# Attention scores as four float32r products of rounded parts and rests over 128 rows, softmax sums divided out of the rows of values, last layer's rows transposed by DMA

## Chip, cores and metric

The kernel runs on one core of one Trainium2 chip, in one launch. The metric is device microseconds of that core. PE is the matrix engine (PEld its weight loads), DVE the vector engine, ACT the scalar engine, POOL the GpSimd engine, SP the queue that issues every DMA.

## What is computed

The reference, cut to what matters:

```python
B, H, S, D = 4, 8, 576, 64
scores = 1 / sqrt(D) * q @ k.T                          # per batch and head, 576x576
kth = the 32nd largest score of each row
attn = exp(where(scores >= kth, scores, -1e9) - max)
attn = attn / (sum(attn) + 1e-9);  out = attn @ v
x = rows of out, heads side by side                      # 2304x512
x = (sigmoid(x @ w_gate) * (x @ w_val)) @ w_out          # 512 -> 1536 -> 512
h = x @ w_in;  solu = h * softmax(h)                     # 512 -> 1024
out = (layer_norm(solu) * g_ln) @ w_out2                 # 1024 -> 512
```

All inputs and the output are float32. The choice of the 32nd largest score makes the scores need close to full float32 precision.

## The kernel before, in words

The 2304 token rows are cut into 18 chunks of 128 rows: per batch four chunks of 128 rows (main), and two chunks that each hold the last 64 rows of two batches (remainder). A chunk's attention is four steps, 72 in all; a step takes two heads of a main chunk, or four heads of 64 remainder rows.

A step goes so. PE makes the scores in two halves of 288 keys (`scores`, L628 for main chunks, L625 for remainder ones) into the PSUM tile ps. The contraction is over 64 rows only: two heads lie in the upper and the lower half of the 128 rows, and their float32 products run at the same time in two (remainder: four) parts of the array. In the trace each float32 product is two records, so a half of a main step is 4 records of L628 and a half of a remainder step 8 of L625. ACT copies ps to s (L634), DVE folds the halves by maximum and minimum (L639, L643) into w and finds the 32nd largest value in four rounds of top eight (L653 MAX8, L657 MATCH_REPLACE8). ACT masks and takes exponentials (L675, L680, with the row sums in sm). POOL adds 1e-9 to the sum (`total1`, L684), DVE inverts it (L688), ACT rounds the normalised row to half precision (`prob_hi`, L701), POOL normalises the row in float32 (`norm`, L693) and subtracts the rounded part (`prob_lo`, L705). One DMA transposes both halves (L712, tile et), and PE multiplies them with the values (`attend`, L727).

After four steps the chunk's sums of values, av, are scaled and split in two float16 parts xt (L753, then L771 on POOL or L764 on DVE). The three dense layers work with three float16 products for each float32 one: gate and value groups pg, pv (L863), px (L909), ph (L946), po (L1044), each in groups of 12 products of 128 columns or 3 of 512. The second rests are made by POOL from a float32 copy in chunks 0 to 3, and by DVE straight from PSUM (`lower`, L764) in chunks 4 to 17, which the constant DIRECT lists. Before the last layer the rows e (128x1024) are turned: PE transposes them in eight float32 blocks (`turn`, L1018, tile pl), ACT and DVE split them (L1023, L764).

The weights come in as doubles and are rebuilt to float32 in the first 150 us by DVE (L424 to L430), ACT and POOL, then split in float16 halves.

The order on each engine is written out by a planner (class Order): every piece of work has an engine, a booked cost, a rank, its needs, and buffers that it takes and frees (BUFS gives the number of each). The table SHIFT moves the ranks by key. The planner plays the program through with these costs and issues the instructions in the order found; each engine runs its own list in order. SP has one list too, with loads, transposes and stores in it.

Of the kernel before, what the change touches and what calls it, by code (L numbers as in the profile page):

```python
# [10 lines left out]
F32 = mybir.dt.float32  # L11
F16 = mybir.dt.float16
# [9 lines left out]
P = 128  # L22
# [18 lines left out]
DIRECT = tuple(range(4, 18))  # L41
# [4 lines left out]
BUFS = dict(s=4, ks=5, v=4, q=2, w=4, et=2, ps=1, pt=1, av=1, pm=4, xt=1, gh=1, two=3, big=2, xf=1, x2=1)  # L46
# [9 lines left out]
ADDED = tuple(range(24))  # L56
STAGED = 36
SHIFT = {
# [75 lines left out]
def terms(name):  # L134
# [6 lines left out]
    if k in ("kd", "vd", "vn", "vh", "vl"):  # L141
        return [(k, 1.0), (("b", name[1]), 1.0)]
# [176 lines left out]
def body(ctx, tc, q_main, q_rem, k_dup, v_pad, w_gate, w_val, w_out1, w_in, w_out2, g_ln, out):  # L319
# [251 lines left out]
    for x, ch in enumerate(chunks):  # L571
        ch["x"] = x
# [617 lines left out]
```

## Time and profile before

| | |
|---|---|
| median of 3 runs | 1004.01 us (1003.17 to 1004.04) |
| the profiled execution | 1002.34 us |
| its span, first to last instruction | 1000.6 us |
| mean granted clock of TensorE | 0.973 of full speed |
| PE, PEld busy | 883.0 us (88%), 668.1 us (67%) |
| DVE busy | 865.0 us (86%) |
| ACT busy | 724.4 us (72%) |
| POOL busy | 569.6 us (57%) |
| chain of work that ended last | PE 75%, DVE 13%, ACT 6%, DMA 3% |

The shares are means over three parts: the first 150 us, in which weights are made ready, a long middle in which attention and dense layers run side by side, and a tail of dense layers alone.

### The profile page before, as it was taken

What the parts mean: (1) busy time and instruction counts of PE and PEld (TensorE: products, weight loads), DVE (VectorE), ACT (ScalarE), POOL (GpSimd) and SP (SyncE); (2) the same over time, 40 slices, a digit from 0 to 9 for tenths busy, and PEclk for the clock granted to TensorE, in tenths of its full rate; (3) what the DMA queues carried; (4) which work ended last, traced back from release to release, by engine and by line L of the source; (5) the groups of instructions that cost most, each with busy time, mean ns of one, the idle gap of its engine ahead of it and who ended that gap; (6) DMA issues with size and microseconds to landing.
All of it is one profiled execution on the core that took longest, in us unless ns stands there. A gap on an engine that the chain in (4) does not pass through costs nothing.

```text
span 1000.6 us, 29578 instructions
## 1 busy us (share of the span) xinstructions
PE 883.0 (88%) x12052; PEld 668.1 (67%) x12052; DVE 865.0 (86%) x2321; ACT 724.4 (72%) x1319; POOL 569.6 (57%) x824
## 2 busy tenths in 40 slices
PE   1343249899999999999999999999999999999995
PEld 1112138777786868786877777676868687877962
DVE  7999999999999999999899999999999999823232
ACT  4998999888789878667797776777987677632221
POOL 6876787786657766555475645645673546530000
PEclk9999658999999999999999999999999999999998
DMA  9982565142641433332514433334332224220000
GB/s 339 327 257 66 138 158 126 30 83 65 141 118 38 95 85 58 82 93 75 112 51 76 63 59 84 84 82 106 77 73 61 69 49 83 50 59 4 10 12 21
DMA packets 194200, 91.56 MB, mean 92 GB/s; under 512 B 171792, under 2 KB 181008, under 8 KB 194064
## 3 DMA queue, kind: packets, MB, share of 16 engines
q1 hardware_dynamic: 194064, 89.68, 36.7%
q8 instruction: 94, 1.54, 0.7%
q14 instruction: 42, 0.34, 0.1%
HBM read 42.47 MB, written 4.72 MB: 47 GB/s over the span
## 4 chain that ended last, share of the span: by engine, by line
PE 75%; DVE 13%; ACT 6%; DMA 3%; issue 1%; POOL 1%; SPq 0%; POOLq 0%; ACTq 0%; DVEq 0%
PE pg L863 15%; PE pv L863 14%; PE px L909 12%; PE ph L946 9%; PE po L1044 9%; PE ps L628 8%; PE av L727 6%; DVE m L653 3%; DVE w L657 2%; PE pl L1018 2%; DVE pd L424 1%; DMA raw<-in_w_in_dram 1%; DMA wi<-in_w_gate_dram 1%; DVE pd L427 1%; PE ps L625 1%
## 5 line engine op out<-in xcount | busy, mean ns | idle before, releaser
L653 DVE MAX8 m<-w 128x8 f32<-128x288 f32 (+1 forms) x576 | 328.6, 598 | 0.1
L657 DVE MATCH_REPLACE8 w<-m,w 128x288 f32<-128x288 f32 (+1 forms) x432 | 232.5, 542 | 0.0
L705 POOL TENSOR_TENSOR h<-s,h 128x576 f16<-128x576 f32 x144 | 184.5, 1285 | 3.1 <-POOL nk L662 0.2
L863 PE MATMUL pg<-xt,wg 128*128 128x128 f16 x2592 | 180.1, 222 | 3.2 <-POOL xt L771 2.2
L909 PE MATMUL px<-gh,wo 128*128 128x128 f16 x2592 | 177.7, 219 | 0.0
L863 PEld LDWEIGHTS <-wg 128*128 128x128 f16 x2592 | 158.1, 100 | 22.9 <-issue 12.1
L863 PE MATMUL pv<-xt,wv 128*128 128x128 f16 x2592 | 171.9, 219 | 0.1
L909 PEld LDWEIGHTS <-wo 128*128 128x128 f16 x2592 | 152.0, 98 | 23.0 <-issue 13.4
L863 PEld LDWEIGHTS <-wv 128*128 128x128 f16 x2592 | 152.5, 98 | 20.5 <-issue 9.9
L693 POOL TENSOR_SCALAR s<-s,sm 128x576 f32<-128x576 f32 x144 | 106.7, 745 | 102.2 <-ACT h L701 101.7
L628 PE MATMUL ps<-k,q 64*128 64x288 f32 x512 | 105.3, 488 | 28.9 <-ACT s L634 11.7
L634 ACT ACTIVATE s<-ps 128x576 f32<-128x576 f32 x144 | 92.6, 643 | 50.6 <-PE ps L628 38.0
L675 ACT ACTIVATE s<-s,nk 128x576 f32<-128x576 f32 x144 | 105.3, 767 | 32.5 <-POOL nk L662 32.3
L701 ACT ACTIVATE h<-s,sm 128x576 f16<-128x576 f32 x144 | 107.4, 767 | 20.4 <-DVE sm L688 16.6
L1044 PE MATMUL po<-wo,lt 128*128 128x512 f16 x432 | 119.7, 389 | 0.0
L946 PE MATMUL ph<-wi,x 128*128 128x512 f16 x432 | 119.5, 388 | 0.0
L680 ACT ACTIVATE s<-s,nb 128x576 f32<-128x576 f32 x144 | 110.0, 766 | 1.1 <-POOL nb L669 1.0
L628 PEld LDWEIGHTS ps<-k,q 64*128 64x128 f32 x512 | 42.1, 198 | 67.8 <-issue 21.4
L727 PE MATMUL av<-et,v 128*64 128x128 f16 (+1 forms) x2400 | 77.9, 220 | 6.5 <-ACT v L608 6.0
L727 PEld LDWEIGHTS <-v 128*64 128x64 f16 x2400 | 66.3, 113 | 23.9 <-issue 12.7
L639 DVE TENSOR_TENSOR w<-ps,s 128x576 f32<-128x576 f32 x72 | 54.1, 751 | 26.1 <-ACT s L634 17.5
L684 POOL TENSOR_SCALAR sm<-sm 128x2 f32<-128x2 f32 x72 | 13.8, 191 | 108.9 <-ACT s L680 103.7
(166 smaller groups left out, 1236.9 us busy)
## 6 DMA issues: line engine op xcount, KB each, us to landing
v<-in_v_pad_dram SPq DMA_DIRECT2D x16, 320.0 KB, 4.1
k<-in_k_dup_dram SPq DMA_DIRECT2D x32, 144.0 KB, 3.1
wi<-in_w_gate_dram SPq DMA_DIRECT2D x8, 512.0 KB, 6.0
q<-in_q_main_dram SPq DMA_DIRECT2D x32, 128.0 KB, 3.3
wo<-in_w_val_dram SPq DMA_DIRECT2D x8, 512.0 KB, 7.6
wi<-in_w_out_dram SPq DMA_DIRECT2D x8, 512.0 KB, 5.4
raw<-in_w_in_dram SPq DMA_DIRECT2D x8, 512.0 KB, 4.8
raw<-in_w_out_dram SPq DMA_DIRECT2D x8, 512.0 KB, 4.4
```

What stands on the lines that cost most here:

```text
L628: nc.tensor.matmul(ps[:, t, :S // 2], q[rows, p], kv["k", b, p][rows, keys], start=True, stop=True)
L653: nc.vector.max(st["m8"][:, t, r * 8:r * 8 + 8], ranked(i, r, t))
L657: nc.vector.match_replace(w, steps[i]["m8"][:, t, r * 8:r * 8 + 8], w, LOW)
L680: nc.scalar.activation(w, w, AF.Exp, bias=st["nb"][:, t:t + 1], scale=D ** -0.5, accum_out=st["sm"][:, t:t + 1])
L693: nc.gpsimd.tensor_scalar(w, w, st["sm"][:, t:t + 1], 1.0, op0=OP.mult, op1=OP.mult)
L701: nc.scalar.activation(st["h"][:, 0, t], st["s"][:, t], AF.Copy, scale=st["sm"][:, t:t + 1])
L705: nc.gpsimd.tensor_sub(st["h"][:, 1, t], st["s"][:, t], st["h"][:, 0, t])
L727: nc.tensor.matmul(ch["av"][j * D:(j + 1) * D, p, st["o"]:st["o"] + wd], v, e[:, y * REM:y * REM + wd], start=one and k == (0, 5)[j], stop ...
L863: nc.tensor.matmul(dst, w[a][:, c, f * P:(f + 1) * P], ch["xt"][:, b, c], start=x == 0, stop=x == len(mm) - 1)
L909: nc.tensor.matmul(ch["px"][:, e], wo1h[a][:, f, e * P:(e + 1) * P], ch["gh"][:, b, f], start=y == 0, stop=y == len(DOWN) - 1)
L946: nc.tensor.matmul(ch["ph", nn], ch["x2"][:, a, c], wih[b][:, c, nn * 512:(nn + 1) * 512], start=c == 0 and a == 0 and b == 0, stop=c == K ...
L1044: nc.tensor.matmul(ch["po"], ch["lt"][:, a, f], wo2h[b][:, f], start=y == 0, stop=y == len(FIN) - 1)
```

## The change

1. Scores. Each q tile and k tile is loaded whole, with the same 64 rows in both halves of its 128 rows. ACT rounds it to float32r (`split_q`, `split_k`), POOL subtracts the rounded part from the float32 one (`rest_q` for all 128 rows, `rest_k` for the lower 64). The k tile then holds the rounded part above and the rest below, one q tile twice the rounded part, the other twice the rest. Two float32r products over 128 rows, added up in PSUM, give the four products of parts. A main half step has four of them, a remainder half step eight; no two run in different parts of the array.
2. Softmax sums. `norm` and the scale of `prob_hi` go; the rows of exponentials are split as they are. Per chunk, not per step, POOL and DVE make the eight inverse sums, POOL splits them in float16 halves, and PE spreads them over columns (`spread`, 16 or 32 small products into rb). ACT copies rb (`take_spread`), DVE multiplies the chunk's av with it (`rows_all`), ACT rounds (`rows_hi`), POOL makes the rest.
3. DIRECT shrinks from chunks 4 to 17 to chunks 16 and 17: the rests of x2 go to POOL, after a float32 copy by ACT.
4. Last layer. In chunks 0 to 15 ACT rounds e to float16 (`last_hi`), POOL makes the rest (`last_lo`), and a DMA transposes both (`flip_last`); PE transposes only in chunks 16 and 17.
5. Buffers: s and w go from 4 to 3, and w is shared with the new tile lh; the q tiles are loaded per step. The table SHIFT is new throughout.

```diff
-DIRECT = tuple(range(4, 18))
+DIRECT = (16, 17)
-BUFS = dict(s=4, ks=5, v=4, q=2, w=4, et=2, ps=1, pt=1, av=1, pm=4, ...
+BUFS = dict(s=3, ks=8, v=4, qr=2, qs=3, w=3, et=2, ps=1, pt=1, av=1, pm=4, ...
 SHIFT = {
-    ("w", "g"): -850.7, ("sw", "g"): -415.1, ("wx", "g"): -364.4, ...
+    ("w", "g"): -803.3, ("sw", "g"): -0.6, ("wx", "g"): -337.1, ...
...
+    def load_q(i, t):
+        st["qr", t] = qr = tl(sp, [P, 2, P], F32, f"qr{i}_{t}", "qr")
+        nc.sync.dma_start(qr, q_rem[...] if st["rem"] else q_main[st["b"], st["c"], :, p:p + 2])
+    def split_q(i, t):
+        st["qs", t] = qs = tl(sp, [P, 2, 2, P], F32R, f"qs{i}_{t}", "qs")
+        nc.scalar.activation(qs[:, 0], st["qr", t], AF.Copy)
+    def rest_q(i, t):
+        nc.gpsimd.tensor_sub(qs[:, 1], qr, qs[:, 0].bitcast(F32))
+    def split_k(b, p, j):
+        kv["k", b, p, j] = ks = tl(sp, [P, S], F32R, f"ks{b}_{p}_{j}", "ks")
+        nc.scalar.activation(ks, kv["raw", b, p, j], AF.Copy)
+    def rest_k(b, p, j):
+        nc.gpsimd.tensor_sub(ks[D:], kr[D:], ks[D:].bitcast(F32))
 def scores(i, n):
-            for t in range(2):
-                rows = slice(t * D, t * D + D)
-                    nc.tensor.matmul(ps[:, t, :S // 2], q[rows, p], kv["k", b, p][rows, keys], start=True, stop=True)
+        for t in range(2):
+            mm = [(hl, st["qs", t][:, hl, x] if st["rem"] else st["qs", 0][:, hl, t], p) for x, p in enumerate(st["pairs"]) for hl in range(2)]
+            for y, (hl, q, p) in enumerate(mm):
+                nc.tensor.matmul(ps[:, t, :S // 2], q, kv["k", b, p, t][:, keys], start=y == 0, stop=y == len(mm) - 1)
...
-    def norm(i, t):
-        nc.gpsimd.tensor_scalar(w, w, st["sm"][:, t:t + 1], 1.0, op0=OP.mult, op1=OP.mult)
+    def inverse_halves(ch):
+        nc.gpsimd.tensor_scalar(ih[:, 0], ch["sm"], 1.0, 1.0, op0=OP.mult, op1=OP.mult)
+        nc.gpsimd.tensor_sub(ih[:, 1], ch["sm"], ih[:, 0])
+    def spread(ch):
+        for y, i in enumerate(ch["steps"]):
+            for x, p in enumerate(st["pairs"]):
+                for a in range(2):
+                    for t in range(2):
+                        nc.tensor.matmul(rb[t * D:t * D + D, p, st["o"]:st["o"] + wd], ch["ih"][:, a, 2 * y + t:2 * y + t + 1].to_broadcast([P, D]),
+                                         ident16[:, rows], start=a == 0, stop=a == 1)
-        nc.scalar.activation(st["h"][:, 0, t], st["s"][:, t], AF.Copy, scale=st["sm"][:, t:t + 1])
+        nc.scalar.activation(st["h"][:, 0, t], st["s"][:, t], AF.Copy)
+    def rows_all(ch):
+        nc.vector.tensor_mul(ch["xf"], ch["av"], ch["xf"])
...
+    def last_hi(ch):
+        ch["lh"] = tl(sp, [P, 2, FF2], F16, "lh", "w")
+        nc.scalar.activation(ch["lh"][:, 0], ch["e"].rearrange("p a b -> p (a b)"), AF.Copy)
+    def last_lo(ch):
+        nc.gpsimd.tensor_sub(ch["lh"][:, 1], ch["e"].rearrange("p a b -> p (a b)"), ch["lh"][:, 0])
+    def flip_last(ch):
+        nc.sync.dma_start(ch["lt"].rearrange("p c k q -> p (c k) q"), ch["lh"].rearrange("p c f -> p (c f)"), transpose=True)
...
-        for nn in range(2):
+        for nn in range(2) if x in LATE else ():
             op(("tu", nn), "PE", 0.455, N + 22, lambda ch=ch, nn=nn: turn(ch, nn), [("l4", x)], take=["pm"],
```

The planner books 0.62 us for a main half step of scores (0.5 before) and 1.16 us for a remainder one.

How the orders change, at three places. PE, a half step of main scores in the middle of the program, among products of the dense layers; before (k and q are the loaded float32 tiles):

```order
L946 LDWEIGHTS x_11739
L946 MATMUL ph<-wi,x_11739 128x512
L628 MATMUL ps_0_12183<-k_2_11150,q_0_11356 128x288 x2
L1044 LDWEIGHTS lt
L1044 MATMUL po<-wo_79,lt 128x512
```

The same engine and the like place now (ks and qs are the float32r tiles of parts):

```order
L894 LDWEIGHTS wv
L894 MATMUL pv<-xt_9761,wv 128x128
L645 MATMUL ps_0_10391<-ks_2_0_7948,qs_0_9797 128x288 x2
L645 MATMUL ps_0_10391<-ks_2_1_8001,qs_0_9797 128x288 x2
L894 LDWEIGHTS wg
L894 MATMUL pg<-xt_9761,wg 128x128
```

Two products at the same time became four one after the other, two for each head. POOL, about one step of the middle, before (nk, nb are the threshold and the span of a step, s its row, h its halves):

```order
L684 TENSOR_SCALAR sm_7157<-sm_7157 128x2
L693 TENSOR_SCALAR s_6713<-s_6713,sm_7157 128x576 x2
L705 TENSOR_TENSOR h_7242<-s_6713,h_7242 128x576 x2
L662 TENSOR_SCALAR nk_7359<-m_7140 128x2
L668 TENSOR_TENSOR nb_7364<-m_7140 128x2
```

and now:

```order
L615 TENSOR_TENSOR ks_1_0_7733<-kr_1_0_7688,ks_1_0_7733 64x576
L736 TENSOR_TENSOR h_7740<-s_7272,h_7740 128x576
L603 TENSOR_TENSOR qs_0_7655<-qr_0_7431,qs_0_7655 128x256
L736 TENSOR_TENSOR h_7740<-s_7272,h_7740 128x576
L679 TENSOR_SCALAR nk_7817<-m_7690 128x2
L684 TENSOR_TENSOR nb_7826<-m_7690 128x2
```

The two normalisations of a step are gone, and the rests of q and k tiles stand between the rests of the rows. DVE, the first product of gate and value (chunk 0), before (m and w belong to top-eight rounds):

```order
L653 MAX m_1374<-w_1343 128x8 x2
L657 MATCH_REPLACE w_1343<-m_1374,w_1343 128x576 x2
L653 MAX m_1374<-w_1343 128x8
L688 RECIPROCAL sm_1514<-sm_1514 128x2
L889 SCALAR_TENSOR_TENSOR sg<-sg,pv 128x512
```

and now:

```order
L430 SCALAR_TENSOR_TENSOR pd<-raw,pd 128x512
L660 TENSOR_TENSOR w_1490<-ps_1_1233,s_1217 128x2x288
L433 SCALAR_TENSOR_TENSOR wo_81<-raw,pd 128x512
L670 MAX m_1508<-w_1490 128x8
L920 SCALAR_TENSOR_TENSOR sg<-sg,pv 128x512
```

It stood behind 63 MAX instructions and 50 rebuilt weight pieces, and stands now behind 51 and 48; the next chunks' first products stand behind 95, 127 and 159 MAX instructions (before: 91, 135 and 162).

## Rows read from the trace of the kernel before

**Rows 1.** Windows: length; busy us of PE, PEld, DVE, ACT, POOL; clock; DMA share.

```profile
0.00:150.00 150.00, 51.36 (x346) 30.78 (x348) 138.26 (x324) 125.22 (x206) 111.31 (x122) 0.87 0.70 214
150.00:250.00 100.00, 94.77 (x1405) 77.83 (x1402) 96.25 (x264) 85.95 (x152) 75.06 (x102) 0.95 0.35 76
250.00:950.00 700.00, 699.06 (x10012) 536.98 (x10010) 615.42 (x1696) 501.06 (x940) 381.39 (x595) 1.00 0.33 73
950.00:1001.00 51.00, 37.77 (x299) 22.47 (x296) 15.05 (x38) 12.19 (x23) 1.86 (x6) 0.93 0.04 16
```

**Rows 2.** Timeline of PE: start, us, records, idle before; main scores among 128-column products.

```profile
351.42 0.83 PE L863 MATMUL pv<-xt,wv 128*128 128x128 f16 x12
352.09 0.83 PE L863 MATMUL pg<-xt,wg 128*128 128x128 f16 x12
352.85 0.76 PE L628 MATMUL ps<-k,q 64*128 64x288 f32 x4
353.54 2.19 PE L863 MATMUL pv<-xt,wv 128*128 128x128 f16 x36
```

**Rows 3.** Timeline of PE: a remainder half step of scores.

```profile
254.30 0.78 PE L863 MATMUL pv<-xt,wv 128*128 128x128 f16 x11
255.01 0.71 PE L625 MATMUL ps<-k,q 64*64 64x288 f32 x8
255.66 1.03 PE L727 MATMUL av<-et,v 128*64 128x128 f16 x30
```

**Rows 4.** Timeline of PE: products with values, then 512-column groups.

```profile
355.66 1.03 PE L727 MATMUL av<-et,v 128*64 128x128 f16 x30
356.62 0.85 PE L863 MATMUL pv<-xt,wv 128*128 128x128 f16 x12
357.30 0.84 PE L1044 MATMUL po<-wo,lt 128*128 128x512 f16 x3
357.98 0.84 PE L946 MATMUL ph<-wi,x 128*128 128x512 f16 x3
```

**Rows 5.** Timeline of PE: four float32 transposes among 128-column products.

```profile
386.81 0.55 PE L863 MATMUL pg<-xt,wg 128*128 128x128 f16 x7
387.25 0.66 PE L1018 MATMUL pl<-ident,e 128*128 128x128 f32 x4
387.75 0.83 PE L863 MATMUL pg<-xt,wg 128*128 128x128 f16 x12
```

**Rows 6.** Groups by line, weight loads: count, busy us, mean ns, idle before.

```profile
L863 PEld LDWEIGHTS <-wv 128*128 128x128 f16 x2592 | 152.5, 98 | 20.5 <-issue 9.9
L1018 PEld LDWEIGHTS pl<-ident,e 128*128 128x128 f32 x144 | 16.1, 146 | 12.0 <-issue 9.6 <-POOL e L1013 0.7 <-DVE e L1010 0.5
```

**Rows 7.** Groups by line, POOL, ACT and DVE.

```profile
L693 POOL TENSOR_SCALAR s<-s,sm 128x576 f32<-128x576 f32 x144 | 106.7, 745 | 102.2 <-ACT h L701 101.7
L705 POOL TENSOR_TENSOR h<-s,h 128x576 f16<-128x576 f32 x144 | 184.5, 1285 | 3.1 <-POOL nk L662 0.2
L612 POOL TENSOR_TENSOR v<-tv,v 128x320 f16<-128x320 f32 x32 | 27.6, 875 | 4.0 <-ACT v L608 3.8
L771 POOL TENSOR_TENSOR xt<-xf,xt 128x512 f16<-128x512 f32 x4 | 4.6, 1160 | 2.6 <-ACT xf L753 2.6
L753 ACT ACTIVATE xt<-av,fr_y 128x256 f16<-128x256 f32 x4 | 1.7, 463 | 0.1
L701 ACT ACTIVATE h<-s,sm 128x576 f16<-128x576 f32 x144 | 107.4, 767 | 20.4 <-DVE sm L688 16.6 <-issue 2.4 <-ACT s L634 0.9
L998 ACT ACTIVATE junk<-e,st 128x1024 bf16<-128x1024 f32 x18 | 20.6, 1144 | 18.4 <-DVE st L991 18.3
L764 DVE SCALAR_TENSOR_TENSOR lt<-pl,lt 128x512 f16<-128x512 f32 x28 | 19.0, 683 | 25.0 <-ACT lt L1023 25.0
```

**Rows 8.** Windows around the last top-eight round, same columns as rows 1.

```profile
862.00:873.00 11.00, 11.00 (x159) 9.43 (x156) 10.86 (x31) 6.48 (x12) 4.59 (x6) 1.00 0.24 55
873.00:950.00 77.00, 77.00 (x1116) 63.64 (x1114) 23.03 (x55) 26.21 (x48) 13.67 (x21) 1.00 0.10 24
```

More of the change, by code (lines that the diff above doesn't have):

```diff
@@ L11 @@
 F32 = mybir.dt.float32
+F32R = mybir.dt.float32r
 F16 = mybir.dt.float16
@@ L173 @@
                 POOL=(100, 70, 80, 100, 1250), DMA=(0,) * 5)
-    TAKER = dict(s="ACT", ks="DMA", v="DMA", q="DMA", w="DVE", et="DMA", ps="PE", pt="PE", av="PE", pm="PE",
+    TAKER = dict(s="ACT", ks="ACT", v="DMA", qr="DMA", qs="ACT", w="DVE", et="DMA", ps="PE", pt="PE", av="PE", pm="PE",
                  xt="ACT", gh="ACT", two="ACT", big="DMA", xf="ACT", x2="ACT")
@@ L538, in weights @@
             W = (key, f, c)
-            add(("wh", *W), "ACT", 1.48, t + 0.6 * x, lambda f=f, c=c: split_hi(f, c), [("wc", key)], take=["two"])
+            pool = number[f, c] in SCALED
+            add(("wt", *W), *(("POOL", 0.66) if pool else ("ACT", 0.7)), t + 0.6 * x, lambda f=f, c=c: split_hi(f, c), [("wc", key)], take=["two"])
+            add(("wh", *W), "ACT", 0.75, t + 0.6 * x, lambda f=f, c=c: split_first(f, c), [("wt", *W)])
             add(("wl", *W), "POOL", 1.23, t + 0.6 * x, lambda f=f, c=c: split_lo(f, c), [("wh", *W)], free=["two"])
@@ L572, in body @@
         ch["x"] = x
+        ch["steps"] = [i for i, st in enumerate(steps) if st["ch"] is ch]
     kv = {}
@@ L778, in body @@
         t = use[0] * STEP
-        add(("kd", b, p), "DMA", 1.0, t - 3 * STEP, lambda b=b, p=p: load_k(b, p),
-            ([("kd", b, p - 1)] if p else [("kd", b - 1, NPAIR - 1)] if b else []), take=["ks"], delay=0.95)
+        for j in range(2):
+            add(("kd", b, p, j), "DMA", 0.85, t - 3 * STEP, lambda b=b, p=p, j=j: load_k(b, p, j),
+                ([("qk", uses[b - 1, p][-1], 1)] if b else []) + [("kd", b, p, 0)] * j, take=["big"], delay=0.95)
+            add(("kb", b, p, j), "ACT", 0.575, t - 2 * STEP,
+                lambda b=b, p=p, j=j: split_k(b, p, j), [("kd", b, p, j)], take=["ks"])
+            add(("ka", b, p, j), "POOL", 1.37, t - 2 * STEP, lambda b=b, p=p, j=j: rest_k(b, p, j),
+                [("kb", b, p, j)], free=["big"])
         add(("vd", b, p), "DMA", 0.91, t - STEP, lambda b=b, p=p: load_v(b, p), take=["v"], delay=0.95)
@@ L786, in body @@
             add(("vl", b, p, x), "POOL", 0.75, t + STEP, lambda b=b, p=p, x=x: value_lo(b, p, x), [("vh", b, p, x)], free=["two"])
-    for x, ch in enumerate(chunks):
-        ch["steps"] = [i for i, st in enumerate(steps) if st["ch"] is ch]
-        for j in range(len(ch["vs"])):
-            add(("qd", x, j), "DMA", 0.8, ch["steps"][2 * j] * STEP - 3 * STEP, lambda ch=ch, j=j: load_q(ch, j),
-                [("qd", x, j - 1) if j else ("qd", x - 1, len(chunks[x - 1]["vs"]) - 1)] if x or j else [], take=["q"], delay=0.95)
     for i, st in enumerate(steps):
@@ L795, in body @@
         rem, b, ch = st["rem"], st["b"], st["ch"]
-        done_q = st["last"] or rem and ch["steps"].index(i) == 1
+        for t in range(2 if rem else 1):
+            before = [(i, 0)] if t else [(i - 1, int(steps[i - 1]["rem"]))] if i else []
+            add(("qd", i, t), "DMA", 0.47, t0 - 3 * STEP, lambda i=i, t=t: load_q(i, t), [("qd", *x) for x in before], take=["qr"], delay=0.95)
+            add(("qb", i, t), "ACT", 0.31, t0 - 2 * STEP, lambda i=i, t=t: split_q(i, t), [("qd", i, t)] + [("qb", *x) for x in before],
+                take=["qs"])
+            add(("qa", i, t), "POOL", 0.7, t0 - 2 * STEP, lambda i=i, t=t: rest_q(i, t), [("qb", i, t)], free=["qr"])
         for n in range(2):
-            add(("qk", i, n), "PE", 0.5, t0 - STEP, lambda i=i, n=n: scores(i, n),
-                [("qd", ch["x"], st["j"])] + [("kd", b, p) for p in st["pairs"]] + ([("qk", i, 0)] if n else [("qk", i - 1, 1)] if i else []), take=["ps"],
-                free=(["q"] * done_q + ["ks"] * sum(uses[b, p][-1] == i for p in st["pairs"])) * n)
-            add(("se", i, n), "ACT", 0.53, t0 - STEP, lambda i=i, n=n: take_scores(i, n), [("qk", i, n)] + [("se", i, 0)] * n,
+            add(("qk", i, n), "PE", 1.16 if rem else 0.62, t0 - STEP, lambda i=i, n=n: scores(i, n),
+                [("qa", i, t) for t in range(2 if rem else 1)] + [("ka", b, p, t) for p in st["pairs"] for t in range(2)] + ([("qk", i, 0)] if n else [("qk", i - 1, 1)] if i else []),
+                take=["ps"], free=(["qs"] * (2 if rem else 1) + ["ks"] * sum(2 * (uses[b, p][-1] == i) for p in st["pairs"])) * n)
+            add(("se", i, n), "ACT", 0.55, t0 - STEP, lambda i=i, n=n: take_scores(i, n), [("qk", i, n)] + [("se", i, 0)] * n,
                 take=["s"] * (n == 0), free=["ps"] * (n == 0))
@@ L849, in body @@
                     needs.append(("vk", key, bb))
-            cost = 0.57 if len(ch["vs"]) == 1 else 0.8
-            add(("xh", ch["x"]), "ACT", cost, e + 6, lambda ch=ch: rows_hi(ch), needs, take=["xt"])
-            if ch["x"] in DIRECT:
-                add(("xl", ch["x"]), "DVE", 0.6 if len(ch["vs"]) == 1 else 0.75, e + 6, lambda ch=ch: rows_direct(ch), [("xh", ch["x"])], free=["av"])
-            else:
-                add(("xf", ch["x"]), "ACT", cost, e + 6, lambda ch=ch: rows_all(ch), [("xh", ch["x"])], take=["xf"], free=["av"])
-                add(("xl", ch["x"]), "POOL", 1.11, e + 6, lambda ch=ch: rows_rest(ch), [("xf", ch["x"])], free=["xf"])
+            x = ch["x"]
+            add(("iw", x), "POOL", 0.19, e, lambda ch=ch: total1(ch), [("ex", y, t) for y in ch["steps"] for t in range(2)])
+            add(("iv", x), "DVE", 0.08, e, lambda ch=ch: inverse(ch), [("iw", x)])
+            add(("ih", x), "POOL", 0.36, e, lambda ch=ch: inverse_halves(ch), [("iv", x)])
+            add(("rb", x), "PE", 0.46, e + 5, lambda ch=ch: spread(ch), [("ih", x)] + ([("va", x - 1, 7)] if x else []), take=["pm"])
+            add(("rs", x), "ACT", 0.5 if len(ch["vs"]) == 1 else 0.7, e + 5, lambda ch=ch: take_spread(ch), needs[1:] + [("rb", x)], take=["xf"], free=["pm"])
+            add(("xa", x), "DVE", 0.61, e + 6, lambda ch=ch: rows_all(ch), [("at", i), ("rs", x)], free=["av"])
+            add(("xh", x), "ACT", 0.52, e + 6, lambda ch=ch: rows_hi(ch), [("xa", x)], take=["xt"])
+            add(("xl", x), "POOL", 1.12, e + 6, lambda ch=ch: rows_rest(ch), [("xh", x)], free=["xf"])
     def group(ch, dst, w, f):
@@ L1063, in tA, with op @@
             return (4 * x + BEHIND + 4 * a / ATOMS) * STEP
-        def op(name, engine, cost, a, fn, needs=(), take=(), free=(), table=None, delay=0.0, x=x, port=None):
-            add((*name[:1], x, *name[1:]), engine, cost, tA(a), fn, needs, take, free, table, delay, port)
+        def op(name, engine, cost, a, fn, needs=(), take=(), free=(), table=None, delay=0.0, x=x, port=None, room=None):
+            add((*name[:1], x, *name[1:]), engine, cost, tA(a), fn, needs, take, free, table, delay, port, room)
         if ("fs", key) not in order.ops:
@@ L1119, in body @@
         N = ATOMS
-        for nn in range(2):
+        if x not in LATE:
+            op(("lh",), "ACT", 0.95, 57, lambda ch=ch: last_hi(ch), [("l4", x)], take=["w"])
+            op(("ll",), "POOL", 2.3, 57, lambda ch=ch: last_lo(ch), [("lh", x)], free=["big"])
+            op(("lr",), "DMA", 3.1, N + 10, lambda ch=ch: flip_last(ch), [("ll", x)], take=["big"], free=["w"], delay=1.5,
+               room=lambda ch=ch: room_last(ch))
+        for nn in range(2) if x in LATE else ():
             op(("tu", nn), "PE", 0.455, N + 22, lambda ch=ch, nn=nn: turn(ch, nn), [("l4", x)], take=["pm"],
```

104 lines of the change are left out of this document (49 added, 55 removed), and 137 rows, old and new, of the table SHIFT.

## Prediction

> **What bounds the kernel now.** I read the windows first. In the first 150 us DVE is busy 138 and PE 51: weights are rebuilt and the first steps ranked, and PE waits for them [rows 1]. From 250 to 950 us PE is busy 699 of 700 us at full clock [rows 1]. DVE has 615 of 700 there, but nearly all that it lacks comes after the last top-eight round: from 873 us on it works 23 of 77 us, while PE goes on at 77 of 77 [rows 8]. So at the end PE is behind, with dense layers left over, and PE's own work sets the end; in the last 51 us it waits 13 us for the chain through the last chunk [rows 1].
>
> A full busy share alone proves little for a pipelined engine, so I read the timeline of PE next. Groups of 12 products of 128 columns start 0.67 us apart (351.42, 352.09), 0.056 us a product, and groups of three products of 512 columns 0.68 apart, 0.227 a product [rows 2, 4]. Both are 0.44 us per 1000 columns: PE takes columns without a break. I count PE time, then, from start to start of groups. The Trainium skill (Perfetto Trace Analysis, Identifying the Most-Contended Engine) warns that matmul busy share says little and wants the busy share of weight loads instead; here that is 537 of 700 us, which would leave PE room. If it had room, the change would pay only what DVE loses (below, some 20 us), about the same sum; the pace of the groups speaks for the columns.
>
> **The scores.** Before: the 12 products from 352.09 end, at their pace, at 352.76; the next group after the scores starts at 353.54. So a main half step costs PE 0.78 us, of which 0.09 is a wait ahead of its first product [rows 2]. A remainder half step costs 0.75: 11 products from 254.30 end at 254.91, and the next kind starts at 255.66 [rows 3]. 128 x 0.78 + 16 x 0.75 = 112 us.
> After: 640 products of 288 columns over 128 rows in float32r, with nothing beside them in the array. The trace has no float32r product, so I bound one.
> - Low end: the pace of the float16 products of 512 columns, 0.227 x 288/512 = 0.128 us [rows 4]; 640 x 0.128 = 82.
> - High end: the float32 transposes, four of 128 columns in 0.50 us (387.25 to 387.75), 0.125 each with all that belongs to them [rows 5]; scaled by columns 0.28 us, 640 of them 180. If half of those 0.125 us is a weight load that does not grow with columns, it is 0.128 + 0.06 = 0.19, or 120.
> I take the low end with one wait of 0.09 for each of the 144 groups: 82 + 13 = 95. The reason: the product is single, without the second record that each float32 product has (4 records of L628 for two products, rows 2), and its 0.128 us of columns are longer than the 0.06 that a float32 weight load can leave open, so the next load fits under it. **Term: 95 - 112 = -17 us**; ends -30 (no waits at all) and +68.
>
> **Weight loads, by the skill.** A float32 weight load shows 146 ns on average, a float16 one 98 [rows 6]. The Trainium skill (TensorE: Matmul & The Clock Gate, Weight-path perf modes) says why: fast weight load needs 128 columns and a type other than float32. The rows agree in direction. By that rule the 640 new loads are all slow ones; if they lay open, the gain would be gone. That is a rival below, priced from rows.
>
> **The transposes.** 128 of 144 leave PE: 32 groups of four. A group costs 0.50 us [rows 5]. **Term: -16 us.** What takes their place is 16 x (one ACT rounding of 1024 columns, two times 0.6 or the 1.14 of L998; a POOL subtraction of 1024 columns, twice 1.16; one DMA transpose) [rows 7]. All of it is queued some microseconds ahead of the last layer's products, while PE has other chunks' groups. If that cover is gone, a late one costs PE about 3 to 6 us in a chunk.
>
> **The spreading of the sums.** 320 small products: 256 of 128 columns into 64 columns of the array, 64 of 64 columns. The nearest row is the product with the values, which has the same shape and also alternates between the two column halves: 30 in 0.96 us (355.66 to 356.62), 0.032 each [rows 4]. 320 x 0.032 = 10, and 18 waits of 0.09 at the change of kind: **term +12 us**; ends +10 and, if they don't run side by side, 320 x 0.056 + 2 = +20 [rows 2].
>
> **DVE, POOL, ACT.** DVE loses 52 subtractions of L764 (28 to 4, 14 to 2, and all 16 of xt), about 50 x 0.68 = 34 us, and 54 small reciprocals; it gains 18 products at about 0.75, 13.5 [rows 7]: -20 or a little more, about as much as PE. POOL loses `norm`, 107 us, and gains 80 rests of q (256 columns: 0.875 x 256/320 = 0.70, so 56), 32 rests of k (1.29 each, 41), 26 subtractions of 512 columns for xt and x2 at 1.16 (30) and 16 of 1024 columns (37) [rows 7]: about +45 on 570. ACT gains 80 roundings of q at 0.46 (37), 32 of k at 0.77 (25), 16 of e (18) and a copy for each chunk, and loses 32 copies of 512 columns, under 0.77 each, some 22 [rows 7]: about +70 on 724. Both stay below DVE's load in the middle (501 and 381 of 700 [rows 1], so some 560 and 415). I book these at nothing on the path; what covers them is PE's backlog. A step's chain gets shorter (no inverse and no `norm`, 2 x 0.75 us between ACT and the transpose), a chunk's longer (spread, copy, product, rounding, rest: some 3 us more), and buffers s and w are 3 in place of 4.
>
> **Start.** In the new order the first gated product stands on DVE behind 12 MAX instructions, with their share of a step and a half, and two weight pieces less. At 0.6 to 0.7 us an instruction that is some 15 us. But the second chunk's stands behind four MAX more, the third's and fourth's behind 8 and 3 less. PE can begin its dense layers earlier and may starve between; 0 to -15. Against it stand waits that the tighter buffers, the fuller ACT and the per-step q loads on SP may put on PE: 0 to +20. I set the two against each other.
>
> **Sum.** -17 - 16 + 12 = -21 from the profiled execution's 1002.3 (span 1000.6): 981. The median of the runs is 1.7 above that execution, so **983 us**.
>
> **Rivals.**
> 1. A float32r product takes two columns' time for each column, as the float32 transposes do if their loads are hidden (0.125 us for 128 columns is 2.2 times the 0.056 of the float16 product [rows 2, 5]): 640 x 0.256 = 164, +52 against before. Then 1004 + 52 - 16 + 12 = 1052, **slower**. The whole change pays nothing from (112 + 4)/640 = 0.18 us a product on. For it: the only single-pass float32 rows of the trace are that slow. Against it: half of their time can be the load.
> 2. The weight loads lie open: 640 x 0.19 = 120, and +8 - 16 + 12 = +4: 1008, slower by a little.
> 3. PE starves. Attention reaches the dense layers later because DVE waits for w, or the SP list stands at a q load while a transposed row is due behind it. One such loss of 0.3 us in each of 72 steps eats the 21: 995 to 1012. For it: DVE was busy 95% up to its last round (615 of 700 less the 34 of rows 8, over 612 us [rows 1, 8]) and has no room to make up. Against it: it has 20 us less to do.
> 4. The early start holds in full, 15 us, and nothing starves: 962 to 972.
> 5. The products run side by side less than I think, or the spreading costs 20: inside the first case's own range, 972 to 994.
>
> **How the numbers follow.** Forecast (972 to 994): 0.54. Rival 4: 0.12. Rival 3: 0.17, half of it under 1002. Rival 2: 0.06. Rival 1: 0.11. The range 962 to 1012 leaves out rival 1 and little else. A measurement of this kernel tells 0.2%, 2 us, from no change. Faster: 0.54 + 0.12 + 0.09 = 0.75; same (1002 to 1006): 0.07; slower: 0.18.
>
> **What would show it.** In the profile of the changed kernel: L645 in the timeline of PE, four records between neighbours 0.55 to 0.65 us apart (0.78 before); above 0.75 the first term is wrong. L723 groups of 16 in 0.5 to 0.6. The windows of PE in the middle at 50 of 50; under 49, rival 3 holds, and the waits of DVE's fold and of PE name the place. The first gate group before 150 us or not tells the start. DVE's total near 845.

## The result, and the profile after

The changed kernel takes 992.51 us (median of 4 runs, 990.38 to 993.9) against 1003.59 for the kernel before: ratio 0.9891, interval 0.9878 to 0.9904. It is 11 us faster; the prediction said 21. The sign and the range held, the size is at the far end of the forecast's own range (972 to 994).

The page of the changed kernel, its span and first section (busy us, share of the span, instructions):

```profile
span 990.5 us, 30262 instructions
PE 872.0 (88%) x12244; PEld 714.2 (72%) x12244; DVE 841.0 (85%) x2234; ACT 750.4 (76%) x1433; POOL 617.4 (62%) x808
```

PE is busy 11 us less than before and DVE 24 us less, ACT 26 us more and POOL 48 us more. The windows that answer to [rows 1], same columns:

```profile
0.00:150.00 150.00, 64.24 (x569) 51.22 (x570) 138.09 (x321) 127.91 (x221) 122.34 (x127) 0.85 0.69 225
150.00:250.00 100.00, 90.55 (x1332) 78.42 (x1331) 99.27 (x264) 86.01 (x165) 69.46 (x95) 0.95 0.49 101
250.00:950.00 700.00, 689.17 (x10158) 568.75 (x10156) 593.70 (x1627) 526.51 (x1031) 423.72 (x581) 1.00 0.43 93
950.00:991.00 41.00, 28.01 (x194) 15.77 (x191) 9.99 (x25) 9.94 (x18) 1.86 (x6) 0.86 0.06 20
```

Three differences are to be seen. PE does 13 us more in the first 150. From 150 to 250 it does 4 us less, and in the middle it is busy 689 of 700, where it was busy 699. The tail is as before: 13 us of idle time.

The terms of the sum can be read from single groups. Timeline of PE: main scores (L645) between products of 128 columns, one remainder half step, the spreading of the sums (L723), and the first group of gate products:

```profile
560.33 0.83 PE L894 MATMUL pv<-xt,wv 128*128 128x128 f16 x12
560.98 0.77 PE L645 MATMUL ps<-ks,qs 128*128 128x288 f32 x4
561.59 0.84 PE L894 MATMUL pv<-xt,wv 128*128 128x128 f16 x12
...
644.75 0.83 PE L940 MATMUL px<-gh,wo 128*128 128x128 f16 x12
645.39 1.30 PE L645 MATMUL ps<-ks,qs 128*128 128x288 f32 x8
646.54 0.66 PE L894 MATMUL pg<-xt,wg 128*128 128x128 f16 x9
...
442.01 0.84 PE L977 MATMUL ph<-wi,x 128*128 128x512 f16 x3
442.77 0.64 PE L723 MATMUL rb<-ident,ih 128*64 128x128 f16 x16
443.35 0.85 PE L977 MATMUL ph<-wi,x 128*128 128x512 f16 x3
...
131.30 3.09 PE L894 MATMUL pg<-xt,wg 128*128 128x128 f16 x36
```

The first group of gate products in the kernel before:

```profile
150.63 7.23 PE L863 MATMUL pg<-xt,wg 128*128 128x128 f16 x84
```

A main half step now costs 0.60 us: the 12 products from 560.33 end, at their pace, at 561.00, and the next kind starts at 561.59. It was 0.78 [rows 2]. A remainder half step costs 1.13 (645.42 to 646.54), it was 0.75 [rows 3]. The spreading costs 0.58 a group, and 0.08 of waiting stand ahead of it (the three products from 442.01 end, at their pace, at 442.69). So the scores' term is 128 x (0.60 - 0.78) + 16 x (1.13 - 0.75) = -17, as forecast. The transposes are gone but for 16 records of L1062, and the spreading costs, with these waits, about 12. **By this count PE's work did shrink by 21 us.** Half of that didn't arrive.

To see where it went I counted PE's work with the pace of each kind at full clock (0.056 us for a product of 128 columns, 0.227 for 512, 0.148 for a product of the new scores with its share of the wait, and so on), stage by stage, and took it from the stage's length. What is left is time that PE spent waiting or at the lower clock. These are estimates; the -1.8 shows that a stage can be off by 2 us:

| stage, us | before | after | difference |
|---|---|---|---|
| 0 to 150 | 122.5 | 113.4 | -9 |
| 150 to 250 | 10.7 | 16.5 | +6 |
| 250 to 950 | -1.8 | 11.8 | +13.5 |
| 950 to the end | 14.4 | 15.2 | +1 |
| PE's work in all | 854.7 | 833.6 | -21 |

The profiled executions took 1002.3 and 992.2 us: -21 of work, -9 in the start, and +20 of new waits. In the start the first gate products come 19 us earlier (131.30 against 150.63). The +20 are the question.

What PE waits for, from 150 to 960 us (total, times, longest), the first lines:

```profile
PE ps L645 <- ACT s L651: 5.3, 12, 0.8
PE ps L645 <- DVE n L375: 2.3, 1, 2.3
PE pg L894 <- POOL xt L798: 1.8, 3, 1.1
```

They are short and of many kinds, and no single one makes up the 20. The whole list of 15 kinds has no transfer in it. DVE shows more. Its list has a long pause in the second remainder chunk, between the 53rd step and the 54th (timeline of DVE; idle time before an instruction and its releaser in brackets):

```profile
655.60 0.21 DVE L1022 TENSOR_SCALAR st<-st 128x1 f32<-128x1 f32 x1
658.60 0.69 DVE L920 SCALAR_TENSOR_TENSOR sg<-sg,pv 128x512 f32<-128x512 f32 x1 [2.79 <-PE pv L894]
664.06 0.16 DVE L372 TENSOR_SCALAR n<-ptot 128x1 f32<-128x1 f32 x1 [4.77 <-PE ptot L388]
...
669.87 0.69 DVE L920 SCALAR_TENSOR_TENSOR sg<-sg,pv 128x512 f32<-128x512 f32 x1 [4.96 <-PE pv L894]
672.86 0.69 DVE L920 SCALAR_TENSOR_TENSOR sg<-sg,pv 128x512 f32<-128x512 f32 x1 [2.30 <-PE pv L894]
677.69 0.76 DVE L656 TENSOR_TENSOR w<-ps,s 128x576 f32<-128x576 f32 x1 [4.15 <-ACT s L651]
```

In these 22 us DVE works about 3, while PE is busy without a break, mostly with dense layers: the second half of this step's scores stands behind them in PE's list, at 675.50. And the last top-eight round now comes later than before, although DVE has 24 us less to do: it starts at 879.09, before it ended at 872.9.

```profile
879.09 0.75 DVE L670 MAX8 m<-w 128x8 f32<-128x576 f32 x1
```

### The profile page after: what moved, and what is told of

It is laid out like the page before. It is cut to its first block, busy times and chain, and to the rows that moved or that the text cites. A ratio compares the mean times of both kernels' runs of the same rounds, so it can differ in the third digit from the quotient of the medians.

```text
span 990.5 us, 30262 instructions
## 1 busy us (share of the span) xinstructions
PE 872.0 (88%) x12244; PEld 714.2 (72%) x12244; DVE 841.0 (85%) x2234; ACT 750.4 (76%) x1433; POOL 617.4 (62%) x808
## 5 line engine op out<-in xcount | busy, mean ns | idle before, releaser
L894 PE MATMUL pg<-xt,wg 128*128 128x128 f16 x2592 | 174.3, 221 | 3.3 <-POOL xt L798 1.8
L894 PEld LDWEIGHTS <-wg 128*128 128x128 f16 x2592 | 153.6, 99 | 6.7 <-issue 3.8
L645 PE MATMUL ps<-ks,qs 128*128 128x288 f32 x640 | 132.7, 335 | 27.5 <-ACT s L651 12.2
L645 PEld LDWEIGHTS ps<-ks,qs 128*128 128x128 f32 x640 | 98.5, 200 | 54.1 <-ACT s L651 20.1
L732 ACT ACTIVATE h<-s 128x576 f16<-128x576 f32 x144 | 96.0, 673 | 1.0 <-DMA lt<-lh 0.9
L758 PEld LDWEIGHTS <-v 128*64 128x64 f16 x2400 | 67.8, 114 | 22.1 <-issue 15.2
L603 POOL TENSOR_TENSOR qs<-qr,qs 128x256 fp32r<-128x256 f32 x80 | 58.5, 735 | 22.5 <-ACT qs L599 22.3
L1088 PEld LDWEIGHTS <-lt 128*128 128x128 f16 x432 | 38.9, 98 | 42.4 <-issue 2.5
```

The source lines that it names most:

```text
L645: nc.tensor.matmul(ps[:, t, :S // 2], q, kv["k", b, p, t][:, keys], start=y == 0, stop=y == len(mm) - 1)
L732: nc.scalar.activation(st["h"][:, 0, t], st["s"][:, t], AF.Copy)
L758: nc.tensor.matmul(ch["av"][j * D:(j + 1) * D, p, st["o"]:st["o"] + wd], v, e[:, y * REM:y * REM + wd], start=one and k == (0, 5)[j], stop ...
L894: nc.tensor.matmul(dst, w[a][:, c, f * P:(f + 1) * P], ch["xt"][:, b, c], start=x == 0, stop=x == len(mm) - 1)
L1088: nc.tensor.matmul(ch["po"], ch["lt"][:, a, f], wo2h[b][:, f], start=y == 0, stop=y == len(FIN) - 1)
```

## The experiments

All are the changed kernel with one edit, if nothing else is said, and its order of instructions is kept. Times are medians; the changed kernel is 992.5.

### Does PE's work still set the time?

**Less work on PE**: the products with the rests of q left out.

```
-  ... for x, p in enumerate(st["pairs"]) for hl in range(2)]
+  ... for x, p in enumerate(st["pairs"]) for hl in range(1)]
```

> The changed kernel with its order kept, but the products with the rests of q are left out (320 of 640 float32r products; the scores lose the rests of q). A product costs 0.13 us from start to start in the trace of the changed kernel, so 42 us of PE work go. Theory (PE's own work sets the end): PE loses 42 us and the time falls by most of it, to 955 to 965 us; what is missing to 950 is new waits of PE. Rival (DVE and ACT, by the pace of attention, set the end already): PE's work turns into PE idle time, 980 to 990 us.

Measured: 988.95 us, ratio to the kernel before 0.9845 (0.9828 to 0.9862). PE lost 42 us of work, and the time fell by 3.5. In the middle PE is busy 667 of 700:

```profile
250.00:950.00 700.00, 667.25 (x9942) 540.54 (x9940) 594.86 (x1630) 526.53 (x1033) 425.22 (x588) 1.00 0.43 93
```

The first of PE's waits in the same window, where the changed kernel has 5.0 us of it:

```profile
PE ps L645 <- ACT s L651: 12.3, 18, 1.6
```

The rival holds: PE now waits where it worked. Below the changed kernel's load, a microsecond of PE's work is worth a twelfth of a microsecond.

**More work on PE**: eight float32 transposes more ahead of the last layer of 16 chunks, as many as the change took away.

```
+            for f in range(8 if ch["x"] not in LATE else 0):
+                nc.tensor.transpose(ch["po"][:, f % 4 * P:(f % 4 + 1) * P], ident, ident)
```

> The changed kernel with its order kept, and eight extra float32 transposes of the identity into po ahead of each last layer of chunks 0 to 15, as PE did there before; the DMA transposes stay. PE work +14 to +16 us. Theory (PE work sets the end, the DMA transposes themselves cost PE nothing): 1004 to 1009 us. Rival (PE has slack in the middle): 992 to 998 us.

Measured: 997.47, ratio 0.9936 (0.9921 to 0.995), in the rival's range. Eight transposes take 0.88 us in its trace, so the 128 are 14 us of work, and the time rose by 5:

```profile
488.69 1.04 PE L1087 MATMUL po<-ident 128*128 128x128 f32 x8
489.56 0.84 PE L1090 MATMUL po<-wo,lt 128*128 128x512 f16 x3
```

**The old products**: the scores by packed float32 products of 64 rows, on the rounded parts alone, with all the roundings and rests still made.

```
-                nc.tensor.matmul(ps[:, t, :S // 2], q, kv["k", b, p, t][:, keys], start=y == 0, stop=...)
+                nc.tensor.matmul(ps[:, t, :S // 2], st["qs", 0][rows, 0, t].bitcast(F32), k, start=True, stop=True)
```

> The changed kernel with its order kept, but its score products are those of before: float32 over 64 rows, two or four at a time in parts of the array, on the rounded parts alone (the scores lose the rests). Theory (the score products pay 17 us of PE work, and PE work sets the end): a main half step costs 0.78 us again and a remainder one 0.75, PE work +17; some of it covers PE's present waits, so 1000 to 1010 us. Rival (the float32r products pay nothing, or PE work does not set the end): 990 to 995 us.

Measured: 1000.6, ratio 0.9972 (0.9959 to 0.9985): +8 for 17 us, the low end of the theory's range. The three runs agree: above the changed kernel's load a microsecond of PE's work is worth a third to a half, and below it far less. My reading that PE's own work sets the end fits the windows of the kernel before (699 of 700); no run took work off that kernel to test it. The changed kernel has left that regime.

### What shares the bound?

**Less work on DVE**: one MATCH_REPLACE of 576 columns in each step left out.

```
-        nc.vector.match_replace(w, ...)
+        if (r, t) != (2, 0): nc.vector.match_replace(w, ...)
```

> The changed kernel with its order, and one MATCH_REPLACE of 576 columns in each of the 72 steps left out (the third of the first row set), so the fourth round ranks some values again: 72 x 0.75 = 54 us less of DVE's work, PE's work as it is. Theory: after the change DVE's list, in order, sets the pace of the steps, and the end follows the last step: 960 to 978. Rival: PE's own work still sets the end alone: 988 to 993. Between the two: both lists hold each other, and each alone gives a part.

Measured: 982.44, ratio 0.9797 (0.9769 to 0.9825): 10 us for 54 us of DVE's work (72 instructions of 0.75; its busy time fell by 43, from 841.0 to 797.6). That is between the theory and the rival, where both lists hold each other.

**Both**: this edit and the one that takes out the rests of q.

```
-  ... for x, p in enumerate(st["pairs"]) for hl in range(2)]
+  ... for x, p in enumerate(st["pairs"]) for hl in range(1)]
-        nc.vector.match_replace(w, ...)
+        if (r, t) != (2, 0): nc.vector.match_replace(w, ...)
```

> The changed kernel with both cuts: the products with the rests of q left out (320 of 640, 42 us of PE's work, which alone gave 3.5 us) and one MATCH_REPLACE in each step (54 us of DVE's work). Theory: PE and DVE are bound together, so with both lighter the time falls by more than the two cuts alone give in sum, to 935 to 960. Rival: a third thing (ACT, the transposes on SP, the order itself) holds the steps, and the two cuts give no more than their sum.

Measured: 969.39, ratio 0.9666 (0.9643 to 0.9688). That is 23 us under the changed kernel, where the two cuts alone give 3.5 + 10 = 13.6. Busy time, first section of its page:

```profile
PE 831.6 (86%) x11924; PEld 670.5 (69%) x11924; DVE 796.5 (82%) x2090; ACT 748.3 (77%) x1433; POOL 616.6 (64%) x808
```

The cuts give more together than apart: PE and DVE hold each other. Still it is 23 of 85 us of busy time (96 by the instructions taken out), less than the theory's 935 to 960. One reason may be that the lists, which fix who waits for whom, were laid out for the full work; no run tests it.

### Is the pause of 22 us the loss?

In the runs up to here the time was always the last top-eight round plus some 110 us: 877 and 988 with less PE work, 888 and 1000 with the old products, 883 and 996 with more transposes (spans). So I thought that whoever brings that round forward moves the end. Two runs on the order alone, with all work in place.

**The second half of the scores one PE group later**, from step 18 on, so that ACT's copy of the first half is out of its way:

```
+    for i in range(18, 72):
+        x = names.index(("qk", i, 1))
+        ...
+        items.insert(stop, items.pop(x))
```

> The changed kernel, with one thing moved in the order: from step 18 on the second half of a step's scores stands one PE group (0.7 us) later in PE's list. PE waits some 5 to 7 us in the middle for ACT's copy of the first half (L645 on L651). Theory (this gate is about half of the 13 us that PE lost in the middle): these waits fall below 2 us and the time by 3 to 6, to 986 to 990 us. Rival (the copy is late because attention as a whole is late, the gate only shows it): DVE's fold starts later, waits turn up at other places, 991 to 997 us.

Measured: 995.42, ratio 0.9913 (0.9899 to 0.9928): 3 us slower, in the rival's range. PE's waits for that copy fall from 5.3 to 2.3 us, but DVE's last top-eight round starts 4.5 us later (883.57 against 879.09). The short waits for ACT's copy are not the loss.

**The steps from the 54th on ahead of dense layers**:

```
+        self.ends, order, self.end = self.play(ops, ahead, [t - ahead_of(n) for n, t in zip(self.ops, self.ends)], True)
+    if k in ("kd", "kb", "ka") and name[1] == 3 or k in ("qk", "se", "fm", "fn", "m", "r", "nk", "nb", "qd", "qb", "qa") and name[1] > 52:
+        return 20000
```

> The changed kernel with all of its work; only the order is laid out once more with the scores, the ranking and the loads of q and k of steps 53 to 71 given a rank 20 us earlier, ahead of dense layers. That closes the hole of about 23 us on DVE between the end of the 53rd and that of the 54th step. Theory: the last round of the ranking plus a tail of 110 us is the end, so the last round 8 to 15 us earlier gives 978 to 985. Rival: the hole is slack, PE has the same work in it and only does dense layers first; the last round comes earlier, the tail grows by as much, and the time is 989 to 997.

Measured: 995.81, ratio 0.9926 (0.9905 to 0.9948). The last round comes 12.5 us earlier:

```profile
866.61 0.75 DVE L670 MAX8 m<-w 128x8 f32<-128x576 f32 x1
```

and the time is 3 us longer, in the rival's range. **The theory falls.** The windows of the pause show how. First the changed kernel, then this one, 650 to 690 us, columns as above:

```profile
650.00:690.00 40.00, 40.00 (x602) 32.79 (x600) 20.11 (x52) 23.12 (x43) 25.61 (x30) 1.00 0.47 111
```

```profile
650.00:690.00 40.00, 38.51 (x567) 31.37 (x563) 25.93 (x68) 30.12 (x58) 32.84 (x39) 1.00 0.53 118
```

DVE does 6 us more here, and PE 1.5 less. In the changed kernel PE was full in the pause: it did dense layers first and scores after. Swapped, they leave the same work, and the tail grows from 111 us to 126. This pause of DVE was no loss, since PE was full in it, and the constant between two events was no cause. Where the 3 us more come from, the run doesn't show.

### The fourth buffers

The change has one more part, which I had passed over: tiles s and w have 3 buffers in place of 4, since the doubled tiles of k and q need the room. The kernel **before**, with that alone (its order laid out once more, with the old order as rank; with the counts left at 4 this gives the old order back, so the counts alone make the difference):

```
+        BUFS.update(s=3, w=3); self.ends, order, self.end = self.play(ops, ahead, list(self.ends), True)
```

> The kernel before with the one edit that tiles s and w have 3 buffers each, as in the changed kernel, in place of 4; its order is laid out once more with the old order as rank. All work is the same. Theory: the changed kernel lost half of its gain because ranked scores and probabilities run less far ahead with one buffer fewer, so PE and DVE wait for each other; then the kernel before gets 5 to 15 us slower by this alone, 1009 to 1019, with more idle time of DVE ahead of its last round. Rival: the fourth buffers were spare, and the loss lies in the longer chain of rounding and subtracting ahead of the scores: 1001 to 1006.

Measured: 1019.62, ratio 1.0163 (1.0141 to 1.0186). **Two buffers fewer cost 16 us** in the kernel before, with the same work, under ranks that were made for four. The windows, to be held against [rows 1]:

```profile
0.00:150.00 150.00, 51.64 (x344) 30.61 (x344) 139.03 (x327) 122.08 (x201) 108.83 (x120) 1.00 0.66 215
150.00:250.00 100.00, 87.49 (x1263) 72.82 (x1264) 88.99 (x242) 80.78 (x144) 70.84 (x94) 0.90 0.34 74
250.00:950.00 700.00, 692.97 (x9909) 529.20 (x9907) 618.33 (x1705) 501.18 (x944) 388.93 (x605) 1.00 0.33 73
950.00:1018.00 68.00, 54.90 (x542) 37.17 (x539) 20.32 (x50) 17.27 (x32) 1.86 (x6) 0.92 0.03 13
```

The pattern resembles that of the changed kernel, but is not the same. Nothing is lost in the start and in the tail. From 150 to 250 us PE is busy 7 us less, with a granted clock of 0.90 there (0.95 before); the changed kernel lost 4, at the old clock. In the middle it is 6 us, where the changed kernel lost 10. One place of it, in the timelines of PE, ACT and DVE:

```profile
190.88 0.76 PE L628 MATMUL ps<-k,q 64*128 64x288 f32 x4
205.93 0.51 PE L628 MATMUL ps<-k,q 64*128 64x288 f32 x2 [0.56 <-ACT s L634]
```

```profile
203.75 0.72 ACT L495 ACTIVATE ts<-wo,gscale 128x512 f32<-128x512 f32 x1
204.51 0.88 ACT L496 ACTIVATE wo<-wo,gscale 128x512 f16<-128x512 f32 x1
205.25 0.63 ACT L634 ACTIVATE s<-ps 128x576 f32<-128x576 f32 x1
```

```profile
201.01 0.17 DVE L688 RECIPROCAL sm<-sm 128x2 f32<-128x2 f32 x1 [2.10 <-POOL sm L684]
208.27 0.76 DVE L639 TENSOR_TENSOR w<-ps,s 128x576 f32<-128x576 f32 x1 [7.09 <-ACT s L634]
```

The first half of a step's scores is in PSUM from 191.6 on. The copy of it into s comes at 205.25; PE waits for it before the second half (205.93), and DVE has nothing to fold: it idles 7 us. ACT itself doesn't idle ahead of the copy: the planner, which counts buffers, has put other work in front of it. So the place shows what the order does; that the missing buffer of s made the order so is argued, and only the run as a whole shows the price. The Trainium skill (Perfetto Trace Analysis, Optimization Strategy) says that a gap that keeps coming back on the engine that should be full can mean too few buffers for the next tile. This run agrees that too few buffers cost time. But what it loses is spread over two stages, 7 us of 100 and 6 of 700, and no repeating gap points to it.

Which of the two tiles is it? The same with s alone at 3, and with w alone at 3:

```
+        BUFS.update(s=3); ...
```

```
+        BUFS.update(w=3); ...
```

> The kernel before with 3 buffers for s and 4 for w; order laid out once more with the old order as rank. With 3 for both it took 16 us more. Theory: s, which holds a step's scores from PE's half step to the probabilities' rests, is the one that holds the steps up: 1011 to 1018. Rival: w, which holds the ranked copy, the probabilities' rounded parts and, in the changed kernel, the last rows too, is as scarce: 1005 to 1011.

> The kernel before with 4 buffers for s and 3 for w; order laid out once more with the old order as rank. Theory (s is the scarce one): 1004 to 1009. Rival (w is as scarce as s): 1010 to 1016.

Measured: 1014.68 for s (ratio 1.0115, 1.0098 to 1.0132), 1016.07 for w (1.0132, 1.0117 to 1.0147). The theory that s is the scarce one falls with the second run: either costs 12 to 13 us alone, and both together only 3 to 4 more. One reading is that s and w stand in one pipeline, whose narrowest place sets the pace; no run shows that.

### The change without its scores

The scores' part buys 17 us of PE's work with two buffers and more work for ACT and POOL. What does that cost in the changed kernel? The counterpart: all other parts of the change, packed float32 products on q and k as loaded, and 4 buffers for s and w. Here the order had to be laid out anew, with ranks of its own.

```
-BUFS = dict(s=3, ks=8, v=4, qr=2, qs=3, w=3, ...
+BUFS = dict(s=4, ks=5, v=4, q=2, w=4, ...
-    def split_q(i, t): ...   def rest_q(i, t): ...   def split_k(b, p, j): ...   def rest_k(b, p, j): ...
-                nc.tensor.matmul(ps[:, t, :S // 2], q, kv["k", b, p, t][:, keys], start=y == 0, stop=...)
+                    nc.tensor.matmul(ps[:, t, :S // 2], q[rows, p], kv["k", b, p][rows, keys], start=True, stop=True)
```

> The change without its part on the scores: packed float32 products on q and k as they are loaded, no rounding and no rests of q and k, and with the room that this leaves 4 buffers each for s and w, as before; the sums divided out and the last rows transposed by DMA stay. The order is laid out anew, with ranks of its own. PE has 17 us more work than in the changed kernel (128 half steps of 0.78 in place of 0.60), ACT and POOL about 60 and 95 us less. Theory: the fourth buffers, which were worth 16 us in the kernel before, pay for about all that the faster products give: 987 to 996, within 5 us of the changed kernel's 992.5. Rival: the scores' part pays its 17 us in full in the changed kernel, and the buffers matter only under the old order: 1004 to 1012.

Measured: 995.36, ratio 0.9925 (0.991 to 0.9939). It has 17 us more of PE's work than the changed kernel and takes 3 us more, in the theory's range.

Since a new order may be lucky or not, the same kernel ran with a second list of ranks:

```
-RANK = (...)
+RANK = (... another list ...)
```

> The kernel of the run with packed float32 scores and 4 buffers for s and w, with the same work and another list of ranks; nothing else differs. It tells how far a newly laid out order alone moves the time. Theory (the 3 us between that run, 995.4, and the changed kernel belong to the work and the buffers, not to the luck of one order): within 3 us of it, 992 to 998. Rival (the order alone is worth as much as the parts that are compared): outside of that, 985 to 990 or 1000 to 1008, and then the comparison says nothing finer than 5 to 10 us.

Measured: 995.93, ratio 0.9942 (0.9923 to 0.9961), in the theory's range. The two orders agree within 1 us. The changed kernel itself ran in one order only, so a part of the 3 us can still be that order's luck. Taken as they stand, **the faster products save 17 us of work and 3 us of time.**

Where do the other 14 go? The run with the old products in the changed kernel has the same PE work as these two, but 3 buffers, all the roundings and rests, and the changed kernel's order, which was made for other costs. It takes 1000.6. So 9 of the 14 are lost at the same buffers, in the same order (17 us of work for 8 of time), and only 5 lie between 3 buffers with the roundings and 4 without them. The middle windows of the two orders with 4 buffers, and then of the run with 3:

```profile
250.00:950.00 700.00, 694.49 (x10097) 527.74 (x10092) 590.15 (x1617) 493.60 (x943) 347.54 (x497) 1.00 0.42 83
250.00:950.00 700.00, 691.76 (x10056) 526.53 (x10049) 588.39 (x1606) 492.04 (x936) 346.80 (x496) 1.00 0.43 82
250.00:950.00 700.00, 691.97 (x10070) 527.04 (x10068) 589.19 (x1612) 525.48 (x1025) 424.04 (x584) 1.00 0.42 93
```

PE is 6, 8 and 8 us short of full there. Counted as in the first table (estimates again, good to some 2 us), PE's waits against the kernel before are, in us:

| run | first 150 us | behind them |
|---|---|---|
| changed kernel | -9 | +20 |
| old products, 3 buffers | -12 | +15 |
| old products, 4 buffers, first order | -17 | +13 |
| old products, 4 buffers, second order | -17 | +15 |
| kernel before, 3 buffers | 0 | +16 |

**At equal work of PE, the fourth buffers, the lighter ACT and POOL and an order of their own save together 5 us in the start and 0 to 2 behind it.** In the start the kernel before lost nothing to its buffers, so the 5 are more likely the roundings and rests or the order; these runs don't tell. And 13 to 15 of the 20 us of new waits are there with 4 buffers too. So the 16 us of the last section are the price of two buffers under the old order. Unless both new orders lose what the buffers give, they are not a share of the changed kernel's waits: its order was laid out for three. What the three runs with old products have in common are the other parts of the change (sums divided out, last rows by DMA, the smaller DIRECT) and new orders; which of these makes the 13 to 15 us, no run shows.

None of the versions with the full computation beat the changed kernel.

## Why the prediction was right in sign and half off in size

- **PE's work sets the time**: the windows of before fit it, and it was the ground for all else. After the change it holds no longer: PE is 11 us short in the middle, and a microsecond of its work is worth a half to a twelfth of one. The Trainium skill (Perfetto Trace Analysis, Identifying the Most-Contended Engine) calls matmul busy time a poor measure of how near the engine is to its limit and recommends, beside the share of peak FLOPs, the busy share of weight loads. The runs differ: the busy time of PE fell from 699 to 689 of 700 as PE got freer, while that of the loads rose from 537 to 569. The scores' loads were busy 42 us before (the row below) and are 98.5 now (the row under "Weight loads"), at the same 200 ns each:

```profile
L628 PEld LDWEIGHTS ps<-k,q 64*128 64x128 f32 x512 | 42.1, 198 | 67.8 <-issue 21.4 <-ACT s L634 18.4 <-PE pn L467 6.9
```

- **Scores, -17**: right, 0.60 us a main half step, inside the 0.55 to 0.65 that I named. A product takes 0.13 us from start to start, 0.15 with its share of the wait; rivals 1 and 2 would have needed 0.256 and 0.19. The wait of 0.09 that I put ahead of each group is not there (the products before end at 561.00, the scores start at 560.98); a little less passes behind the group in its place. That the sum came out so well is partly luck.
- **Weight loads**: they are slow, 200 ns on average in the row below against 98 for float16 [rows 6], and they cost nothing that shows, since the half steps run near the pace of the columns (0.13 us a product against 0.128). The Trainium skill (TensorE: Matmul & The Clock Gate, Weight-path perf modes) gives no fast weight load to float32; the row agrees:

```profile
L645 PEld LDWEIGHTS ps<-ks,qs 128*128 128x128 f32 x640 | 98.5, 200 | 54.1 <-ACT s L651 20.1 <-issue 14.4 <-POOL nk L679 6.9
```

- **Transposes, -16, and spreading, +12**: near enough as work (14 us by the run that put them back, and 0.58 a group of L723 with 0.08 ahead). As time, the 14 us of transposes put back cost 5.
- **DVE near 845**: 841. POOL, which I forecast 45 higher, is 48 higher, though the terms that I listed for it come to 57. ACT, forecast 70 higher, is only 26 higher.
- **Start and waits, set against each other**: this is the step that failed. I gave the start 0 to -15 and the waits 0 to +20 and let them cancel. They came as -9 and +20. What I had priced at nothing is that PE waits more when its own work gets shorter (with 42 us taken out, 38 came back as waits). I booked the extra work of ACT and POOL at nothing because "PE's backlog" covers it, but the backlog was what the change shortened. The runs show that 5 of the 20 us come and go with the 17 us of the scores (+20 against +15 with the old products). The half sentence "buffers s and w are 3 in place of 4" stood without a price too; it is worth 16 us in the kernel before, but the comparison at equal work leaves it 0 to 2 of the 20 here. The cause of the other 13 to 15 stays open.
- **Rival 3** (PE starves, 995 to 1012) was the nearest to what happened, by a loss that I placed at 0.3 us a step; it comes to 20 us over 72 steps, 0.28. It didn't reach its time because the start gave 9 us, which I had left out of it. Of its two grounds, the SP list is not to be seen directly: from 150 us on no transfer ends a wait of PE. DVE's part is, in so far as less work on DVE gains 10 us.
- **Middle windows**: I asked for 50 of 50 and named 49 as the point for rival 3. They came to 49.2 on average, 689 of 700: just above the line that I had drawn for rival 3.

## What to carry to other kernels

Where one engine is full and the next is 85% busy, don't take what comes off the full one as time: here 17 us of its work were worth 8, and the next 42 worth 3.5. Waits are not a fixed sum; they grow as the work that covers them shrinks. A change in buffer counts needs a price, and running the old kernel with the new counts gives one, but under the old order: here 16 us, where the comparison at equal work in the changed kernel, laid out for three, leaves 0 to 2. So compare in the new kernel too before a cause is named. And a pause on a timeline, or a constant distance to the end, is a reason to make an order-only experiment, not a cause.

## What was not expected of the hardware

- A product in float32r of 128 rows and 288 columns fits in 0.13 to 0.15 us, next to float32 weight loads of 200 ns on average: 0.60 us for four with the change of kind. That is near the column pace of the float16 products (0.227 for 512 columns, so 0.128 for 288), though eight float32 transposes of 128 columns take 0.88 us, 0.11 each (the run that put them back).
- Either of two buffer counts from 4 to 3 costs the kernel before 12 to 13 us, both 16: these prices don't add.
- Two orders of the same work, each laid out by its own list of ranks, came out within 1 us of each other (995.4 and 995.9).
